# A decode attention kernel whose first key load is split into sixteen rows and the other 112

## The chip, the core and the metric

The kernel runs on one core of one Trainium2 chip. The metric is the device time of one execution in microseconds. Three runs of the kernel before took 628.09, 628.12 and 628.2 us; their median, 628.12 us, is the time before.

## The reference

The kernel computes attention of one query position over 65,536 cached keys, with 32 query heads in groups of four that share one of eight key/value heads:

```python
B, Hq, Hkv, Sq, Sk, D = 1, 32, 8, 1, 65536, 128      # all bf16
k = jnp.repeat(k, rep, axis=1)                       # rep = 4
v = jnp.repeat(v, rep, axis=1)
scores = jnp.einsum("bhqd,bhkd->bhqk", q, k) * D ** -0.5
p = _softmax(scores, axis=-1)
return jnp.einsum("bhqk,bhkd->bhqd", p, v)
```

All of K and V is read once, 134.2 MB each, and the output is 8 KB.

## The kernel before, in words

**Tiling.** One head's 65,536 keys are four units of 16,384 keys. A unit lies in SBUF as 128 partitions of T = 128 keys each, a key being 128 bf16 numbers (256 bytes), so a unit of K or of V is 4 MB, 32 KB on each partition. Two units are a pair; the sixteen pairs are the sixteen laps of every engine's loop (NP = 16). Of a pair, one partition holds 256 consecutive keys, 64 KB that are contiguous in HBM.

**What an engine does in a lap.** TensorE (PE) transposes K in blocks of eight 128x128 tiles into PSUM (`trb`, L135). VectorE (DVE) and ScalarE (ACT) copy the blocks to SBUF (`ktb`, evictions at L207 and L205). PE multiplies them with the four queries of the head (L144) into a PSUM bank of scores (`qkb`). DVE takes the maximum (L225), GpSimd (POOL) takes it over the partitions (L393), ACT makes the exponentials (L347), and PE multiplies them with V (L162) into `pvb`. The sums are rescaled from unit to unit on DVE. At the end of the last lap the last head's output is scaled, transposed and stored (L305, L191, L339, L448).

**Buffers and loads.** `kbuf` and `vbuf` hold a pair each (64 KB on each partition), `bbuf` holds the second K unit of a pair. All bulk loads are issued by SyncE (SP), in program order and through one queue: K of a pair, then V of it, lap after lap. Before it issues a K load, SP waits for `kfree`; before V, for `vfree`. In laps 1 to 13 K comes as one load of 8 MB into `kbuf`, and POOL and ACT copy its second unit into `bbuf`. In laps 0, 14 and 15 the two units are loaded apart, into `kbuf` and `bbuf`.

**The start, around the change.** In lap 0 SP issues each K unit as two pieces of 64 keys per partition (`K_PIECES = ((64, 64), (64, 64))`, L407 in `pieces`). A piece is 128 rows of 16 KB, one row on each partition, with 64 KB between the starts of two rows in HBM; it is 2 MB. Each piece has a semaphore (`kp0_0` for the first), which the load raises by 16 when it has landed. Behind the four pieces comes V of pair 0, 8 MB in one load (L437). ACT issues the load of the queries (`qsb`, 32 rows of 256 bytes, L372) on its own queue at the same time.

PE begins with 48 small matmuls on the identity (`PE_LEAD`, L184), transposes the queries when they have landed (L186), waits for the f32 identity (`t_if`), and enters its loop, where the first transposition of `kbuf` waits for `kp0_0`.

**The end.** In the last lap, K comes as two pieces for `kbuf` and one load for `bbuf`, and V as a load of 128 keys per partition and four pieces of 73, 38, 13 and 4 (L407). PE takes each piece as it lands.

## Time and profile before

| | |
|---|---|
| median of three runs | 628.12 us (628.09 to 628.2) |
| span of the profiled execution, first to last instruction | 626.9 us |
| median less that span | 1.2 us |
| PE, DVE, ACT, POOL busy | 77%, 50%, 37%, 26% of the span |
| bulk load queue (q1) busy | 99.2% of sixteen DMA engines over the span |
| HBM read | 268.44 MB, 428 GB/s over the span |

The profile gives the span of one profiled execution and no other time of it; what lies before its first and after its last instruction is seen only as the 1.2 us between the span and the median of the runs. In the rows, L numbers are lines of the kernel; a group's row has its busy time, the mean duration, and what ended the idle time ahead of it. "us to landing" of a DMA runs from its issue to the raising of its semaphore, and so includes the time that it stands in the queue behind earlier loads. In the rows of the stages, the columns after each engine's busy time are the granted clock, the DMA share and the GB/s that the DMA engines moved.

### The profile page before, as it was taken

The numbers are of one execution on the slowest core, as the hardware profiler recorded it, in microseconds if no ns is written. First come the engines' busy times: TensorE is split into PE (matmuls) and PEld (weight loads), VectorE is DVE, ScalarE is ACT, GpSimd is POOL, SyncE is SP. The second block draws the span as 40 slices with busy tenths as digits, with TensorE's granted clock in tenths as the row PEclk, the third lists the DMA queues.
The fourth block names the chain that finished last, engine by engine and source line by source line (L and its number), as shares of the span: only waits on it lengthen the run. The fifth ranks groups of instructions, "written<-read, shape, count | busy, mean of one in ns | idle before, by whom it ended". The sixth has DMA issues, their size and how long they took to land. (4 is left out here: it accounts for less than half of the span.)

```text
span 626.9 us, 27931 instructions
## 1 busy us (share of the span) xinstructions
PE 484.6 (77%) x12340; PEld 478.9 (76%) x12340; DVE 315.1 (50%) x699; ACT 228.9 (37%) x445; POOL 159.9 (26%) x124
## 2 busy tenths in 40 slices
PE   5752995959859498694976959679496894999698
PEld 5752995949859498694976959679496894999698
DVE  4620752817537174371734717356183562848274
ACT  2320532615335153341634407245062441624133
POOL 0000704307042070520605115060150702400000
PEclk9965875958769587695966959678596785969597
DMA  8999999999999999999999999999999999999997
GB/s 366 440 449 424 439 431 439 431 439 426 443 422 447 410 460 410 460 406 460 410 439 431 426 443 426 443 426 439 431 439 431 439 431 435 416 447 424 420 433 302
DMA packets 6280, 268.57 MB, mean 428 GB/s; under 512 B 896, under 2 KB 1024, under 8 KB 1152
## 3 DMA queue, kind: packets, MB, share of 16 engines
q1 hardware_dynamic: 6224, 268.45, 99.2%
q8 instruction: 6, 0.10, 0.1%
q10 hardware_dynamic: 48, 0.01, 0.0%
q14 instruction: 2, 0.02, 0.0%
HBM read 268.44 MB, written 0.01 MB: 428 GB/s over the span
## 5 line engine op out<-in xcount | busy, mean ns | idle before, releaser
L207 DVE COPY ktb<-trb 128x1024 bf16<-128x1024 bf16 x384 | 254.6, 689 | 177.5 <-PE trb L135 173.7
L205 ACT ACTIVATE ktb<-trb 128x1024 bf16<-128x1024 bf16 x128 | 131.0, 1023 | 352.7 <-PE trb L135 297.9
L135 PE MATMUL trb<-ident,kbuf 128*128 128x128 bf16 x2048 | 177.1, 245 | 104.7 <-PEq L49 104.6
L135 PEld LDWEIGHTS trb<-ident,kbuf 128*128 128x128 bf16 x2048 | 143.9, 111 | 105.6 <-issue 105.5
L213 POOL COPY bbuf<-kbuf 128x2048 bf16<-128x2048 bf16 x78 | 143.9, 1893 | 177.6 <-POOLq L49 177.6
L144 PE MATMUL qkb<-qcur,ktb 128*128 128x4 bf16 x4096 | 174.3, 165 | 11.8 <-PEq L49 10.3
L144 PEld LDWEIGHTS qkb<-qcur,ktb 128*128 128x128 bf16 x4096 | 155.2, 97 | 14.6 <-issue 14.6
L135 PE MATMUL trb<-ident,bbuf 128*128 128x128 bf16 x2048 | 157.0, 220 | 5.2 <-issue 3.9
L162 PE MATMUL pvb<-pts,vbuf 128*128 128x4 bf16 x4096 | 113.0, 166 | 15.2 <-PEq L49 11.0
L162 PEld LDWEIGHTS pvb<-pts,vbuf 128*128 128x128 bf16 x4096 | 111.1, 103 | 16.6 <-issue 15.6
L135 PEld LDWEIGHTS trb<-ident,bbuf 128*128 128x128 bf16 x2048 | 117.4, 97 | 5.5 <-issue 5.5
L393 POOL PARTITION_ALL_REDUCE cmaxa<-cmax x32 | 11.9, 370 | 254.1 <-POOLq L49 254.1
L347 ACT ACTIVATE pts<-qkb,negm 128x128 bf16<-128x128 f32 x128 | 50.9, 549 | 37.2 <-ACTq L49 37.2
L356 ACT ACTIVATE bbuf<-kbuf 128x2048 bf16<-128x2048 bf16 x26 | 49.5, 1902 | 0.0
L347 ACT ACTIVATION_READ_ACCUMULATOR pts<-qkb,negm 128x1 f32 x128 | 35.6, 278 | 0.0
L225 DVE TENSOR_REDUCE cmax<-qkb 128x4 f32<-128x512 f32 x32 | 22.0, 686 | 23.4 <-DVEq L49 23.4
L259 DVE TENSOR_TENSOR acc<-acc,pvb 128x4 f32<-128x4 f32 x16 | 2.5, 158 | 30.0 <-PE pvb L162 30.0
L257 DVE COPY acc<-pvb 128x4 f32<-128x4 f32 x8 | 1.3, 163 | 21.8 <-PE pvb L162 21.8
L395 POOL PARTITION_ALL_REDUCE la<-lp x8 | 3.4, 430 | 30.7 <-POOLq L49 30.7
L236 DVE SCALAR_TENSOR_TENSOR negm<-cmaxa,m 128x4 f32<-128x4 f32 x24 | 3.9, 163 | 11.7 <-DVEq L49 11.5
L351 ACT ACTIVATE alpha<-dm 128x4 f32<-128x4 f32 x32 | 7.1, 221 | 0.0
L250 DVE TENSOR_TENSOR acc<-acc,alpha 128x4 f32<-128x4 f32 x24 | 3.9, 164 | 6.1 <-DVEq L49 5.7
(44 smaller groups left out, 41.6 us busy)
## 6 DMA issues: line engine op xcount, KB each, us to landing
kbuf<-in_k_dram SPq DMA_DIRECT2D x4, 2048.0 KB, 16.3
bbuf<-in_k_dram SPq DMA_DIRECT2D x2, 4096.0 KB, 20.9
bbuf<-in_k_dram SPq DMA_DIRECT2D x2, 2048.0 KB, 19.9
kbuf<-in_k_dram SPq DMA_DIRECT2D x1, 4096.0 KB, 16.3
vbuf<-in_v_dram SPq DMA_DIRECT2D x1, 4096.0 KB, 21.9
vbuf<-in_v_dram SPq DMA_DIRECT2D x1, 2336.0 KB, 27.1
vbuf<-in_v_dram SPq DMA_DIRECT2D x1, 1216.0 KB, 29.6
vbuf<-in_v_dram SPq DMA_DIRECT2D x1, 416.0 KB, 30.1
```

Of the source, the lines that this page charges most:

```text
L135: ins = pe.transpose(trb[j % NTB][:, i * P:(i + 1) * P], kv[:, t, :], ident[:, :])
L144: ins = pe.matmul(qkb[n][:, t * R:(t + 1) * R], lhsT=ktb[:, off:off + P], rhs=qcur[:, :], start=True, stop=True)
L162: ins = pe.matmul(pvb[n][:, 0:R], lhsT=vv[:, t, :], rhs=pts[n][:, t * R:(t + 1) * R], start=t == 0, stop=t == T - 1)
L205: e.activation(dst, trb[j % NTB][:, :], AF.Copy).then_inc(eva, 1)
L207: e.tensor_copy(dst, trb[j % NTB][:, :]).then_inc(evd, 1)
L213: ins = op(bbuf[:, c * CB * D:(c + 1) * CB * D], kbuf[:, off:off + CB * D])
L225: e.tensor_reduce(cmax[:, :], qkb[n][:, :].rearrange("p (t g) -> p g t", g=R), AX.X, ALU.max).then_inc(cm, 1)
L236: return e.scalar_tensor_tensor(to[:, :], cmaxa[:, :], -scale, mo[:, :], ALU.mult, ALU.min)
L347: ins = e.activation(pv[:, g, :], sv[:, g, :], AF.Exp, bias=negm[:, g:g + 1], scale=scale, accum_out=rsum[:, g:g + 1])
L351: e.activation(alpha[:, :], dm[:, :], AF.Exp, scale=1.0).then_inc(sx, 1)
L356: return e.activation(o, i, AF.Copy)
L393: e.partition_all_reduce(cmaxa[:, :], cmax[:, :], P, bass.bass_isa.ReduceOp.max).then_inc(cma, 1)
```

## The change

The first piece of `kbuf` in lap 0 is issued as two loads. The first has rows (partitions) 0 to 15, 256 KB, and raises a new semaphore `kf0`; the second has rows 16 to 127, 1.75 MB, and raises `kp0_0`. Both have rows of 16 KB as before. The second piece of 64 keys is issued as before behind them. PE waits for `kf0` once, ahead of its loop, and has one identity matmul less at its start (47 for 48).

```diff
-PE_LEAD = 48
+PE_LEAD = 47
...
+FIRST = 16
...
+    kf0 = sem("kf0")
...
         pe.wait_ge(t_if, 1)
+        pe.wait_ge(kf0, 16)
         with pe.Fori(0, NP) as lap:
             pe_pair(pe, lap)
...
-                    if p == 0 or (p == NP - 1 and n == 0):
+                    if p == 0 and n == 0:
+                        w = K_PIECES[0][0] * D
+                        e.dma_start(to[0:FIRST, 0:w], s[0:FIRST, 0:w]).then_inc(kf0, 16)
+                        e.dma_start(to[FIRST:P, 0:w], s[FIRST:P, 0:w]).then_inc(kp[0][0], 16)
+                        pieces(to[:, w:W], s[:, w:W], K_PIECES[0][1:], kp[0][1:])
+                    elif p == 0 or (p == NP - 1 and n == 0):
                         pieces(to, s, K_PIECES[n], kp[n])
```

On SP's queue these are the first loads before; shapes are partitions x bf16 elements of a row:

```order
L407 DMA kbuf<-in_k_dram 128x8192 x2
L407 DMA bbuf<-in_k_dram 128x8192 x2
L437 DMA vbuf<-in_v_dram 128x32768
L418 DMA kbuf<-in_k_dram 128x32768 [waits kfree]
L437 DMA vbuf<-in_v_dram 128x32768 [waits vfree]
```

And these are the same place of SP's queue in the changed kernel:

```order
L430 DMA kbuf<-in_k_dram 16x8192
L431 DMA kbuf<-in_k_dram 112x8192
L410 DMA kbuf<-in_k_dram 128x8192
L410 DMA bbuf<-in_k_dram 128x8192 x2
L445 DMA vbuf<-in_v_dram 128x32768
L421 DMA kbuf<-in_k_dram 128x32768 [waits kfree]
```

One load of 128 rows has become one of 16 and one of 112; every load behind them stands one issue later, and nothing else on SP's queue moves.

On PE these are the first rows before, with the waits in brackets:

```order
L184 MATMUL pvb<-ident 4x4 [waits t_id]
L184 MATMUL pvb<-ident 4x4 x47
L186 MATMUL pvb<-ident,qsb 128x32 [waits q_sem]
L188 UNCONDITIONAL_BRANCH [waits t_if]
L135 MATMUL trb<-ident,kbuf 128x128 [waits kp0_0]
```

And in the changed kernel:

```order
L186 MATMUL pvb<-ident 4x4 [waits t_id]
L186 MATMUL pvb<-ident 4x4 x46
L188 MATMUL pvb<-ident,qsb 128x32 [waits q_sem]
L191 UNCONDITIONAL_BRANCH [waits kf0,t_if]
L137 MATMUL trb<-ident,kbuf 128x128 [waits kp0_0]
```

The new wait stands on the branch into the loop, directly ahead of the wait for `kp0_0` that was there before. On the other engines the order is the same.

## The prediction

> **What bounds the kernel now.** I read the page's head and its DMA rows first, to see whether any compute engine could be the limit.

> ```profile
> span 626.9 us, 27931 instructions
> ...
> PE 484.6 (77%) x12340; PEld 478.9 (76%) x12340; DVE 315.1 (50%) x699; ACT 228.9 (37%) x445; POOL 159.9 (26%) x124
> ...
> q1 hardware_dynamic: 6224, 268.45, 99.2%
> ```

> No compute engine is over 77%, and the queue of bulk loads keeps the sixteen DMA engines at 99.2% of the whole span. Next I read the stages, to see whether that holds from the first microseconds on.

> ```profile
> core 0: us, PE busy (x) PEld busy (x) DVE busy (x) ACT busy (x) POOL busy (x), PEclk, DMA share, GB/s
> ...
> 1.60:3.60 2.00, 0.34 (x14) 0.34 (x15) 1.21 (x9) 1.21 (x3) 0.00 (x0) 1.00 0.91 264
> 3.60:8.60 5.00, 1.63 (x47) 1.45 (x43) 0.59 (x4) 0.04 (x1) 0.00 (x0) 1.00 1.02 433
> ...
> 20.00:600.00 580.00, 448.18 (x11423) 443.18 (x11421) 289.62 (x631) 214.60 (x415) 157.99 (x115) 0.76 1.00 433
> ```

> From 3.6 us on the loads run at 433 GB/s, and still at 433 as a mean from 20 to 600 us, at a DMA share of 1.00. Only the first two microseconds of transfer are slower, 264 GB/s. One DMA engine therefore moves 433/16 = 27.1 GB/s, and a row of 16 KB takes it 16,384/27.1 = 0.605 us. This **row time** is the unit of what follows. A piece of 128 rows gives each engine eight of them, 4.84 us.

> Does the queue ever run empty, so that a delay at the start could be made up? The issues of the later loads answer that.

> ```profile
> vbuf<-in_v_dram SPq DMA_DIRECT2D x15, 26.8
> kbuf<-in_k_dram SPq DMA_DIRECT2D x13, 25.9
> ```

> These are loads of 8.39 MB, which need 8.39/0.433 = 19.4 us. They land 25.9 and 26.8 us after their issue (medians), so each stands some 6.5 to 7.4 us, less landing itself, behind older loads. There is no empty time into which a late start could vanish.

> Last, what the end hangs on. The chain that ended last, its first pieces and then the stretch that releases it:

> ```profile
> 620.88 2.08 PE pvb L162 x73
> 622.96 0.43 PE pvb L155 x2
> 623.39 1.59 PE pvb L162 x55
> ```
> ```profile
> 579.88 0.33 SPq L428 DMA_DIRECT2D bbuf<-in_k_dram  x1
> ```
> ```profile
> L428 SPq DMA_DIRECT2D bbuf<-in_k_dram x1: 328/328/328, 579.9 to 579.9; - x1
> ...
> DMA to landing us min/median/max: 25.1/25.1/25.1
> ```
> ```profile
> 605.28 0.61 PE L135 MATMUL trb<-ident,bbuf 128*128 128x128 bf16 x8 [1.36 <-PEq L49]
> ```

> The last K load, issued at 579.88, lands at 579.88 + 25.1 = 605.0. PE has stood idle for 1.36 us and takes up `bbuf` at 605.28; the end comes 21.6 us later, through sixteen blocks of K, the exponentials and the values.

> ```profile
> vbuf<-in_v_dram SPq DMA_DIRECT2D x1, 128.0 KB, 29.9
> ```
> ```profile
> 592.83 2.23 SPq L407 DMA_DIRECT2D vbuf<-in_v_dram  x5
> ```

> The last piece of V, issued last of the five at about 594.6, lands at about 594.6 + 29.9 = 624.5, half a microsecond before PE's last matmul ends at 623.39 + 1.59 = 624.98. Both arrivals come off the same queue. So the rule for this case is: **the time moves by as much as the slowest DMA engine falls behind or gets ahead in the first piece**, one for one.

> **The change part by part.** First the edits that I cost at nothing, with what hides them.

> ```profile
> 0.72 0.88 SPq L407 DMA_DIRECT2D kbuf<-in_k_dram  x2
> ...
> 3.26 1.34 PE L184 MATMUL pvb<-ident 128*4 128x4 bf16 x48 [3.26 <-DVE ident L325]
> ...
> 5.03 0.20 PE L186 MATMUL pvb<-ident,qsb 32*128 32x32 bf16 x1 [0.43 <-DMA qsb<-in_q_dram]
> ...
> 8.18 3.57 PE L135 MATMUL trb<-ident,kbuf 128*128 128x128 bf16 x32 [2.94 <-PEq L49]
> ```

> - *One more issue on SP.* Two issues took 0.88 us, 0.44 each. The four loads behind come 0.44 us later, and the 112 rows follow the 16 by 0.44 us. A first row takes each engine at least 0.605 us and the 112 rows another seven row times, 4.2 us, so there is always something queued: 0. Without that cover it would be 0.44.
> - *One identity matmul less.* 1.34/48 = 28 ns, ahead of a wait of 0.43 us for the queries: 0.
> - *The wait for kf0.* It stands ahead of the wait for `kp0_0`, whose 112 rows are issued later: PE is idle for 2.94 us there until 8.18 us, and only blocks of PE's loop are queued behind it. All that PE does next needs `kp0_0` too: 0. PE's own start may slip with the piece, and its idle share (23%) takes that.

> What is left is the transfer. The trace has no bulk load that covers fewer than 128 partitions, so the price of sixteen rows on sixteen neighbouring partitions must be bounded.

> - *Lower end.* If sixteen engines write sixteen neighbouring partitions as freely as 128, the 16 rows take one row time and the 112 rows seven: 0.605 + 4.235 = 4.84, as before. Loss 0. A gain could only come from the slow start: 2.0 us at 264 GB/s instead of 433 is 2.0 x (1 - 264/433) = 0.78 us lost now, and an earlier first row can win back at most that.
> - *Upper end.* The 27.1 GB/s may be the limit not of an engine but of a way into SBUF that serves eight partitions, one engine to each in a load of 128 rows. Then sixteen neighbouring rows may lie on as few as two of the sixteen ways: eight row times each, while the other ways rest. A way that rests still has its eight rows of the piece to receive, and nothing later is slack, so all the rest is lost: 8 x 0.605 = 4.84 us.
> - *Value taken.* The nearest rows lie at the ends, so I take the middle, 2.42 us, which is what four ways would cost (16/4 = 4 row times).

> [...]

> - *The 112 rows.* Seven to an engine no longer fit eight to a way, so two engines will at times write over one way, and such a row goes at half speed. From below 0, as in every 128-row load; from above, all seven rows at half speed, 7 x 0.605 = 4.2 us. I take one row time, 0.6, since the rows seen are all at full speed.
> - *The start itself.* Between 0 and -0.78; I take 0, since each engine still waits for a first row of 16 KB.

> **Sum.** 626.9 + 2.42 + 0.6 = 629.9 us of span; with the 1.2 us that lie around it, 631.1. The same 3.0 us on the median of the runs gives 628.12 + 3.02 = **631.1 us**.

> **The rivals.**

> 1. *The earlier start wins (not slower).* A load of sixteen rows is described sooner than one of 128, each engine has its first row at once, and the ways are no limit. For it: the 264 GB/s of the first two microseconds. Against it: what is slow there may be the first access itself. Price 0 to -0.78, so 627.3 to 628.1, say 627.9. It decides if the 16 rows land in less than about 3.1 us. That bound comes from this row of the loads of `kbuf` up to 12 us:

> ```profile
> DMA to landing us min/median/max: 7.3/9.5/11.7
> ```

> The first piece lands 7.3 us after its issue; less seven row times that leaves 7.3 - 4.24 = 3.1 us. With four shared ways it is 3.1 + 3 x 0.605 = 4.9 us.

> 2. *Shared, but wide.* If neighbours share eight ways, or a way is twice as fast as an engine, the loss is one row time: 628.12 + 0.6 = 628.7, up to 629.3 with a collision.

> 3. *The 112 rows are dealt out in turn.* The one load of few partitions that the trace has is that of the queries:

> ```profile
> qsb<-in_q_dram ACTq DMA_DIRECT2D x1, 8.0 KB, 4.3
> ```

> If neighbouring rows go to neighbouring engines, every round of sixteen rows lies on the same few ways: eight rounds of four row times, 19.4 us instead of 4.84, loss 14.5: 642.6. Against it, weakly: the 32 rows of the queries landed in 4.3 us, but 8 KB would not show a shared way.

> 4. *The loads are not spread as said.* If the 112 rows go to fewer engines, eight say, each has fourteen row times: 8.5 instead of 4.24, loss 4.2: 632.4.

> **How the numbers follow.** Forecast, shared ways with a loss of 1.3 to 4.9: 0.57 (629.4 to 633.0). Rival 1: 0.18. Rival 2: 0.13. Rival 3: 0.06. Rival 4: 0.06. A measurement of this kernel can tell about 0.2%, 1.26 us, from no change. Slower by more than that: forecast, rivals 3 and 4, 0.69. Within it: rival 2 and nearly all of rival 1, 0.29. Faster by more: 0.02, since 0.78 us is the most that the start holds. The range 627.6 to 633.0 takes in the forecast, rivals 2 and 4 and most of rival 1; the forecast's own is 629.4 to 633.0.

> **What would show it.** In the changed kernel the load of 256 KB should land about 4.9 us after its issue (3.1: rival 1). PE's first transposition of `kbuf`, now at 8.18, should come at about 11.2; the GB/s from 1.6 to 3.6 us should fall below 264; from 20 us on 433 must stand; and the last K load should land at about 608 instead of 605.0. I am wrong in the mechanism if the early windows are as fast as before and the end is late all the same, and wrong in size if the 16 rows land at 4.9 but the 112 take longer than eight row times behind them.

## The result, and the profile after

The changed kernel took 631.93 us (five runs, 631.6 to 632.07); the kernel before took 628.12 on the same chip (628.02 to 628.24). The ratio is 1.0059, with a 95% interval of 1.0047 to 1.0071: 3.8 us slower. The prediction was 631.1 with a range of 627.6 to 633.0.

The head of the page of the changed kernel, and its bulk queue:

```profile
span 630.6 us, 27931 instructions
...
PE 486.0 (77%) x12339; PEld 480.7 (76%) x12339; DVE 315.0 (50%) x699; ACT 228.8 (36%) x445; POOL 159.9 (25%) x124
...
q1 hardware_dynamic: 6240, 268.45, 99.2%
```

The span is 3.7 us longer, and these rows do not say where: the busy times of the compute engines differ by at most 1.8 us, and the queue is still "busy" 99.2% of sixteen engines' span. Only the page's row of GB/s in forty slices shows the place: the first slice has 269 for the 366 before. The DMA share does not show it either: in the second of the stages below it is 0.92 at little more than half the rate (243 GB/s for the 433 before). So the rate has to be read beside the share, in the stages of the changed kernel:

```profile
1.60:3.60 2.00, 0.34 (x14) 0.34 (x15) 1.21 (x9) 1.21 (x3) 0.00 (x0) 1.00 1.32 224
3.60:8.60 5.00, 1.18 (x41) 0.97 (x36) 0.59 (x4) 0.04 (x1) 0.00 (x0) 1.00 0.92 243
8.60:11.60 3.00, 0.00 (x0) 0.00 (x0) 0.00 (x0) 0.00 (x0) 0.00 (x0) 1.00 0.93 268
...
20.00:600.00 580.00, 449.56 (x11432) 444.96 (x11429) 290.25 (x632) 213.85 (x414) 157.99 (x115) 0.76 1.00 433
```

Up to 11.6 us the DMA engines move 224 to 268 GB/s at a DMA share of 0.92 or more; before, the window from 3.6 to 8.6 us had 433. From 20 us on it is 433 in both. The loads of the first piece, by their sizes, with the time from issue to landing, and PE's first transposition:

```profile
kbuf<-in_k_dram SPq DMA_DIRECT2D x1, 1792.0 KB, 10.9
kbuf<-in_k_dram SPq DMA_DIRECT2D x1, 256.0 KB, 4.7
```
```profile
12.19 2.08 PE L137 MATMUL trb<-ident,kbuf 128*128 128x128 bf16 x18 [6.34 <-PEq L50]
```

The sixteen rows land 4.7 us after their issue (the prediction had 4.9 for four shared ways, 3.1 for free ones). The 112 rows, issued at 1.2, land at 12.1, and PE starts at 12.19 instead of 8.18: 4.0 us late. What becomes of that is read at the end, from the last K load and the chain that ended last:

```profile
L436 SPq DMA_DIRECT2D bbuf<-in_k_dram x1: 328/328/328, 584.2 to 584.2; - x1
...
DMA to landing us min/median/max: 24.5/24.5/24.5
```
```profile
608.93 0.61 PE L137 MATMUL trb<-ident,bbuf 128*128 128x128 bf16 x8 [0.83 <-PEq L50]
```
```profile
624.53 2.09 PE pvb L164 x73
626.61 0.43 PE pvb L157 x2
627.04 1.57 PE pvb L164 x55
```

The last K load lands at 584.2 + 24.5 = 608.7, where it was 605.0: 3.7 us late. PE takes it up at 608.93 (605.28 before) and the chain ends as far behind. Of the 4.0 us by which PE starts late 3.7 are left at the end. The queue was never empty, as the medians of the 8 MB loads, unchanged to the tenth, show:

```profile
vbuf<-in_v_dram SPq DMA_DIRECT2D x15, 26.8
kbuf<-in_k_dram SPq DMA_DIRECT2D x13, 25.9
```

### The profile page after: what moved, and what is told of

Its sections match the earlier page's. It is cut to its first block, busy times and chain, and to the rows that moved or that the text cites. A ratio compares the mean times of both kernels' runs of the same rounds, so it can differ in the third digit from the quotient of the medians.

```text
span 630.6 us, 27931 instructions
## 1 busy us (share of the span) xinstructions
PE 486.0 (77%) x12339; PEld 480.7 (76%) x12339; DVE 315.0 (50%) x699; ACT 228.8 (36%) x445; POOL 159.9 (25%) x124
## 3 DMA queue, kind: packets, MB, share of 16 engines
q1 hardware_dynamic: 6240, 268.45, 99.2%
## 5 line engine op out<-in xcount | busy, mean ns | idle before, releaser
L137 PE MATMUL trb<-ident,kbuf 128*128 128x128 bf16 x2048 | 179.5, 247 | 107.3 <-PEq L50 107.3
L137 PEld LDWEIGHTS trb<-ident,kbuf 128*128 128x128 bf16 x2048 | 145.5, 112 | 108.3 <-issue 108.1
L146 PEld LDWEIGHTS qkb<-qcur,ktb 128*128 128x128 bf16 x4096 | 156.3, 97 | 14.5 <-issue 14.5
L164 PE MATMUL pvb<-pts,vbuf 128*128 128x4 bf16 x4096 | 112.7, 166 | 15.3 <-PEq L50 11.2
L239 DVE SCALAR_TENSOR_TENSOR negm<-cmaxa,m 128x4 f32<-128x4 f32 x24 | 3.9, 163 | 11.7 <-DVEq L50 11.5
## 6 DMA issues: line engine op xcount, KB each, us to landing
vbuf<-in_v_dram SPq DMA_DIRECT2D x1, 2336.0 KB, 27.1
kbuf<-in_k_dram SPq DMA_DIRECT2D x1, 1792.0 KB, 10.9
```

The costliest lines, as they stand in the source:

```text
L137: ins = pe.transpose(trb[j % NTB][:, i * P:(i + 1) * P], kv[:, t, :], ident[:, :])
L146: ins = pe.matmul(qkb[n][:, t * R:(t + 1) * R], lhsT=ktb[:, off:off + P], rhs=qcur[:, :], start=True, stop=True)
L164: ins = pe.matmul(pvb[n][:, 0:R], lhsT=vv[:, t, :], rhs=pts[n][:, t * R:(t + 1) * R], start=t == 0, stop=t == T - 1)
L239: return e.scalar_tensor_tensor(to[:, :], cmaxa[:, :], -scale, mo[:, :], ALU.mult, ALU.min)
```

## The experiments

Every edit below is in SP's code for the first piece of `kbuf` in lap 0, against the changed kernel, unless said otherwise. Each ran beside the kernel before.

### The same two sizes, cut by columns

```diff
-e.dma_start(to[0:FIRST, 0:w], s[0:FIRST, 0:w]).then_inc(kf0, 16)
-e.dma_start(to[FIRST:P, 0:w], s[FIRST:P, 0:w]).then_inc(kp[0][0], 16)
+c = FIRST // 2 * D
+e.dma_start(to[:, 0:c], s[:, 0:c]).then_inc(kf0, 16)
+e.dma_start(to[:, c:w], s[:, c:w]).then_inc(kp[0][0], 16)
```

> The first piece of 2 MB is again issued as two loads, of 256 KB and 1.75 MB, but cut by columns: 128 rows of 2 KB, then 128 rows of 14 KB. Theory (shared ways: the loss comes from loads that cover few or unevenly many partitions): both loads cover all 128 partitions, so no loss: 628.1 us, within 0.5, at most 0.78 earlier. Rival A (what costs is the extra load itself: its issue, its descriptors, its completion): as the changed kernel, about 631.9. Rival B (HBM reads: what costs is which rows of HBM are read together): the rows read together are those of the kernel before, so 628.1 as well; this run does not tell B from the theory.

Measured: 628.33 us beside 628.2, ratio 1.0 (0.9991 to 1.0009). A second load of 256 KB ahead of the rest costs nothing when it covers all partitions; the extra issue and the wait for `kf0` are in this run as well. Nor does it gain anything. Its early stages:

```profile
1.60:3.60 2.00, 0.34 (x14) 0.34 (x15) 1.20 (x9) 1.21 (x3) 0.00 (x0) 1.00 0.95 307
3.60:8.60 5.00, 1.38 (x44) 1.27 (x40) 0.59 (x4) 0.04 (x1) 0.00 (x0) 1.00 1.01 423
```

The first window is faster than before (307 GB/s for 264), the next one slower (423 for 433), and PE starts at 8.33 instead of 8.18.

### Eight loads of sixteen neighbours, and eight of sixteen spread partitions

```diff
+for i in range(8):
+    r = slice(i * FIRST, (i + 1) * FIRST)
+    e.dma_start(to[r, 0:w], s[r, 0:w]).then_inc(kf0 if i < 7 else kp[0][0], 16)
```

> The first piece is issued as eight loads of sixteen neighbouring rows. Theory: each load lies on four of sixteen ways, so it takes four row times of 0.605 us; eight of them 19.4 us instead of 4.84: 628.1 + 14.5 = 642.6 us. Rival A (each extra load costs 3.8 us, as the one extra load of the changed kernel): 628.1 + 7 x 3.8 = 654.7. If rows of few partitions were free and only the 112 rows cost: 628.1 to 629.

```diff
-    e.dma_start(to[r, 0:w], s[r, 0:w]).then_inc(kf0 if i < 7 else kp[0][0], 16)
+    e.dma_start(to[i:P:8, 0:w], s[r, 0:w]).then_inc(kf0 if i < 7 else kp[0][0], 16)
```

> As the eight loads of sixteen rows, with the same rows read from HBM in the same order, but written to partitions i, i+8, i+16 and so on. The keys then lie on other partitions than their values, so the output is another one; the bytes moved are the same. Theory: sixteen partitions at a step of eight reach eight ways, two rows each, so a load takes two row times, eight loads 9.7 us instead of 4.84: 628.1 + 4.8 = 633.0 us. Rival B (HBM reads): the reads are those of the run beside it, so the same time as that one. Rival A: 654.7, as that one.

Measured: 639.94 us for the neighbours (ratio 1.0192, 1.0176 to 1.0207), 633.16 for the spread ones (1.0079, 1.0064 to 1.0094), beside 628.2. So +11.7 and +5.0. The two differ in nothing but the partitions that they write; the same rows are read from HBM in the same order. That is against rival B, and against rival A too, which had 654.7 for both. The spread loads came out as the theory had it (4.8). The neighbours lost less than the 14.5 that it gave. One stage from the middle of those loads:

```profile
6.00:16.00 10.00, 0.15 (x1) 0.04 (x1) 0.59 (x4) 0.00 (x0) 0.00 (x0) 1.00 0.98 120
```

Sixteen rows are 262 KB, at 120 GB/s 2.18 us, where four row times are 2.42. The kind of cost is right and its size is 10% too high for these loads, of which each lies on other partitions than the one before it.

### The time of a load by its shape

```diff
+for c in cols:                      # the kernel before, ahead of its first load; c: a quarter of vbuf
+    e.dma_start(vbuf[0:P, c], vq[0:P, c]).then_inc(probe, 16)
+e.wait_ge(probe, 64)
+for c in cols:
+    e.dma_start(vbuf[16:P, c], vq[16:P, c]).then_inc(probe, 16)
+e.wait_ge(probe, 128)
...
```

> Ahead of the kernel before, SP issues nine groups of four loads of 16 KB rows into quarters of vbuf (all overwritten later) and waits for each group; the time of one load of a group is (landing of the fourth less landing of the first) / 3. Theory, row time 0.605 us: 128 rows 4.84 us; 112 rows (partitions 16 to 127) about 6.8, as the changed kernel's trace shows; the same 112 partitions from contiguous HBM rows 6.8 too; 112 rows on partitions 0 to 111 also over 4.9; 64 rows on partitions 0 to 63 4.84 (eight ways); 32 rows on 0 to 31 2.42 (eight ways); 16 rows on 0 to 15 2.42 (four ways); 16 rows at a step of eight 1.21; 64 rows at a step of two between 2.42 and 4.84. Without shared ways: 128 rows 4.84, 112 4.24, 64 2.42, 32 1.21, 16 0.605, whatever the step. Rival B (HBM reads): the 112 rows from contiguous HBM take another time than the 112 rows 64 KB apart, and 16 rows take the same at both steps.

> Again groups of four loads of 16 KB rows ahead of the kernel before; the time of one load is (landing of the fourth less landing of the first) / 3. The question is why 112 rows take 6.7 us where the fullest way has only eight rows to take, 4.84. Theory C: the rows are dealt to the engines in runs of neighbours, so that engines meet on a way while other ways rest. Worked through by hand for such runs with ways shared evenly: 112 rows about 6.4 (6.7 was measured), 96 rows on partitions 0 to 95 6.4, 96 on 32 to 127 7.3, 48 on 0 to 47 4.6 to 4.84. Theory D: only the fullest way counts, and 112 has a cost of its own: 96 rows 4.84 both times, 48 rows 4.84. No shared ways: 3.63, 3.63, 1.8. Controls by the ways alone: 32 rows at a step of four on all partitions 1.21 to 2.42; 64 rows on 64 to 127 4.84 to 5.0, as on 0 to 63; 64 odd rows 2.42, as the even ones; 16 rows at a step of four on partitions 0 to 63 1.21 (eight ways).

The rows of three of the groups in the first of these runs (128 rows, 112 rows, 16 rows on partitions 0 to 15) give the first and last issue of the four, then the shortest and the longest time to landing:

```profile
L419 SPq DMA_DIRECT2D vbuf<-in_v_dram x4: 412/416/694, 0.7 to 2.1; - x4
...
DMA to landing us min/median/max: 7.3/13.9/20.5
```
```profile
L422 SPq DMA_DIRECT2D vbuf<-in_v_dram x4: 342/428/483, 22.7 to 24.0; - x4
...
DMA to landing us min/median/max: 8.9/18.8/27.7
```
```profile
L437 SPq DMA_DIRECT2D vbuf<-in_v_dram x4: 311/420/421, 148.6 to 149.9; - x4
...
DMA to landing us min/median/max: 4.7/7.7/10.0
```

These two runs (one execution each) took 807.14 and 762.36 us in all, as the groups stand ahead of everything else. For 112 rows the first lands at 22.7 + 8.9 = 31.6 and the fourth at 24.0 + 27.7 = 51.7, so one takes 20.1/3 = 6.7 us. All groups, worked out in the same way, in us for one load:

| rows of 16 KB on partitions | free rows would take | measured |
|---|---|---|
| 128: all | 4.84 | 4.87 |
| 64: 0 to 63; 64 to 127 | 2.42 | 5.03; 5.03 |
| 64: even; odd | 2.42 | 2.43; 2.43 |
| 32: 0 to 31 | 1.21 | 2.43 |
| 32: every fourth of 128 | 1.21 | 1.40 |
| 16: 0 to 15 | 0.605 | 2.20 |
| 16: every eighth of 128; every fourth of 0 to 63 | 0.605 | 1.23; 1.20 |
| 112: 16 to 127; 0 to 111 | 4.24 | 6.70; 6.73 |
| 112: 16 to 127, rows contiguous in HBM | 4.24 | 6.97 |
| 96: 0 to 95; 32 to 127 | 3.63 | 6.73; 6.80 |
| 48: 0 to 47 | 1.82 | 5.33 |

The fourth load of a group, with none of its group behind it, lands sooner than the others in some groups, so some of these means are low: the landings of the sixteen rows on 0 to 15 are 2.41, 2.41 and 1.78 us apart, those of the 112 rows on 16 to 127 are 7.01, 7.03 and 6.08. In the changed kernel itself the 112 rows land at 1.2 + 10.9 = 12.1 and the sixteen at 0.7 + 4.7 = 5.4, 6.7 apart.

The last three columns of stages in the middle of five of the groups (128; 112; 64 on partitions 0 to 63; 32 on 0 to 31; 64 even) say the same as rates:

```profile
6.00:18.00 12.00, 0.00 (x0) 0.00 (x0) 0.09 (x1) 0.00 (x0) 0.00 (x0) 1.00 1.02 436
30.00:46.00 16.00, 0.00 (x0) 0.00 (x0) 0.00 (x0) 0.00 (x0) 0.00 (x0) 1.00 1.01 278
...
116.00:132.00 16.00, 0.00 (x0) 0.00 (x0) 0.00 (x0) 0.00 (x0) 0.00 (x0) 1.00 1.01 207
138.00:146.00 8.00, 0.00 (x0) 0.00 (x0) 0.00 (x0) 0.00 (x0) 0.00 (x0) 1.00 1.04 215
...
170.00:177.00 7.00, 0.00 (x0) 0.00 (x0) 0.00 (x0) 0.00 (x0) 0.00 (x0) 1.00 1.01 433
```

Partitions 0 to 63 take rows at 207 GB/s and 0 to 31 at 215, half the rate of all 128, while 64 even partitions take them at 433, with the same rows of HBM read as for 0 to 63. It is not how many partitions a load has but which. In row times of 0.605 us, sixteen neighbours (0 to 15) take four where the four loads stand in the queue together (2.41 us from landing to landing), 32 (0 to 31) take no more (2.43), 64 (0 to 63) about eight (5.03), and all 128 no more than those 64 (4.87). The controls go the same way: 0 to 63 at the rate of 0 to 31, the even partitions at the full rate, sixteen at a step of eight nearly twice as fast as sixteen neighbours (1.23 for 2.20). All of these but the even partitions, for which it gave a range, are within 10% of what the theory had by its counts of ways; that rows meet on ways is inferred from these times.

The 112 rows take 6.7 us from HBM rows 64 KB apart and 6.97 from contiguous ones, so the reads do not make them slow. And they take more than the fullest way needs by the theory (eight rows, 4.84). The 96 rows do so too, twice: that is nearer to theory C of the second run (6.4 and 7.3 expected, 6.73 and 6.80 measured) than to D (4.84 both times), but the 0.9 us by which the two were to differ is not there. The 48 rows took 5.33, above what either gave.

The packets kept in the trace, one to a row of 16 KB, go against C as well. In the middle of the group of 128 rows each takes 0.61 us, and in that of 0 to 63 between 1.25 and 1.29, near the two row times (1.21) of the theory. Of the 271 that start in the stage of the 112 rows (30 to 46 us) none is under 0.70 or over 1.40, and half are under 0.93; in the middle of the groups of 96 rows none is under 0.95, and in that of 48 rows each takes 1.78 to 1.92. If engines met on some ways while the others ran free, with each way shared evenly, over half of the rows in a load of 112 or 96 would meet nobody and take about 0.6: that is an estimate, worked out from the row time and runs of neighbours. So all engines are slowed about alike, and C has a sum that is nearly right without the picture behind it.

### The sixteen rows alone

```diff
+spare = sb("spare", [P, 64 * D], DT.bfloat16)
...
-e.dma_start(to[0:FIRST, 0:w], s[0:FIRST, 0:w]).then_inc(kf0, 16)
-e.dma_start(to[FIRST:P, 0:w], s[FIRST:P, 0:w]).then_inc(kp[0][0], 16)
+e.dma_start(spare[0:FIRST, 0:w], s[0:FIRST, 0:w]).then_inc(kf0, 16)
+e.dma_start(to[:, 0:w], s[:, 0:w]).then_inc(kp[0][0], 16)
```

> The load of sixteen rows stays ahead, but into a spare buffer that nothing reads, and the piece itself comes as one load of 128 rows: the sixteen rows are moved twice, and no load has 112 rows. Theory: the sixteen rows cost 2.1 to 2.4 us on their four ways (2.12 was one row's time in the run of eight such loads), and the 128 rows nothing more: 628.2 + 2.1 to 2.4 = 630.3 to 630.6 us. Without shared ways the extra row of each engine costs 0.6: 628.8. If the sixteen rows were the whole loss of the changed kernel, 628.2 + 3.8 + 0.6 = 632.6.

Measured: 630.2 us beside 628.24, ratio 1.0036 (1.0022 to 1.005), +1.96, just under what the theory had. One row more for each engine is 0.605 by the row time, so the sharing of ways by the sixteen rows is put at 1.96 - 0.605 = 1.36 us, an estimate. It is only a part of the 3.8.

### Halves, and even and odd partitions

```diff
+e.dma_start(to[0:64, 0:w], s[0:64, 0:w]).then_inc(kf0, 16)
+e.dma_start(to[64:P, 0:w], s[64:P, 0:w]).then_inc(kp[0][0], 16)
```

> The first piece as two loads of 64 rows, partitions 0 to 63 and 64 to 127. Theory: each half lies on eight of the sixteen ways, eight rows to a way, 4.84 us each (5.0 in the run of shapes): 628.2 + 4.5 to 5.0 = 632.7 to 633.2 us. Rival A (a load that covers fewer than 128 partitions costs something of its own, whichever they are): the same time as the run with even and odd partitions.

```diff
+e.dma_start(to[0:P:2, 0:w], s[0:P:2, 0:w]).then_inc(kf0, 16)
+e.dma_start(to[1:P:2, 0:w], s[1:P:2, 0:w]).then_inc(kp[0][0], 16)
```

> The first piece as two loads of 64 rows, even partitions and odd partitions: the same two loads, rows and bytes as the halves, but each load reaches all sixteen ways with four rows each. Theory: 2 x 2.42 = 4.84, no loss: 628.2 us within 0.4. Rival A: as the halves, 633.

Measured: 633.4 us for the halves (ratio 1.0084, 1.0067 to 1.01), 628.5 for even and odd (1.0004, 0.9995 to 1.0013), beside 628.24. Two loads of 64 rows each, the same bytes, issues and waits: +5.2 and +0.3. Rival A is out. The 5.2 is what the table gives, 2 x 5.03 - 4.87 = 5.19.

### The 112 rows as seven loads at a step of seven

```diff
-e.dma_start(to[FIRST:P, 0:w], s[FIRST:P, 0:w]).then_inc(kp[0][0], 16)
+for i in range(7):
+    r = slice(FIRST + i, P, 7)
+    e.dma_start(to[r, 0:w], s[r, 0:w]).then_inc(kf0 if i < 6 else kp[0][0], 16)
```

> The sixteen rows stay ahead as in the changed kernel; the other 112 rows come as seven loads of sixteen rows at a step of seven, partitions 16, 23, ..., 121, then 17, 24, ..., 122, and so on. A load of sixteen rows gives one row to each engine, so each engine gets a run of seven neighbouring partitions, one after the other. Theory C (the load of 112 rows is dealt to the engines in such runs, and its loss is engines meeting on a way): each engine then has the same rows in the same order as in the changed kernel, so the same time, 631.9 us within 0.5, though there are seven loads instead of one. If 112 rows had a cost of their own, these seven loads would not have it: a load reaches ten or more ways with at most two rows on one, so with engines free to run ahead between 4.84 and 8.5 us for the seven, and nothing that ties it to 6.7. If the 112 rows were dealt in turn, this order would be far better than theirs, which their 6.7 us already speaks against. Rival A (each extra load costs): 628.2 + 7 x 3.8 = 654.8.

Measured: 632.04 us beside 628.21, ratio 1.0058 (1.0045 to 1.0072); the changed kernel's was 1.0059. The stages from 3.6 to 11.6 us are those of the changed kernel (243 and 268 GB/s there):

```profile
3.60:8.60 5.00, 1.19 (x41) 0.98 (x37) 0.60 (x4) 0.05 (x1) 0.00 (x0) 1.00 0.93 243
8.60:11.60 3.00, 0.00 (x0) 0.00 (x0) 0.00 (x0) 0.00 (x0) 0.00 (x0) 1.00 0.97 262
```

Here the deal is made in the program: if the sixteen rows of each load go to the sixteen engines in order, which no view shows, an engine gets seven neighbouring partitions one after the other. That it costs the same as the one load of 112 rows, to 0.1 us, speaks against a cost of 112 rows in one load and for one part of theory C, that the load is dealt in runs of seven neighbours, though the 4.84 to 8.5 us expected without that hold 6.7 as well. It does not show how the loss comes about: the rows are slowed alike here too (none under 0.72 us from 4 to 11 us).

## Why the prediction was right, and what it mis-sized

- **What bounds it**: right, and "one for one" nearly so. Of the 4.0 us by which the first piece came late 3.7 were left at the last K load and in the span.
- **The edits at nothing**: right. The run cut by columns has the additional issue, the wait and the 47 matmuls, and costs nothing that can be measured.
- **Shared ways**: right in kind. Loads that differ only in the partitions that they write go from +5.0 to +11.7 us; even and odd partitions against halves, which also group the reads in another way, from +0.3 to +5.2. Of the signs that were named, the sixteen rows landed at 4.7 us (4.9 forecast), the first window fell to 224 GB/s, PE's first transposition came at 12.19 us (about 11.2 forecast), 433 stood from 20 us on, and the last K load landed at 608.7 (about 608 forecast).
- **The sum** is where the size was off, by 0.8 us: +3.0 forecast, +3.8 measured. The time of the first piece was forecast as four row times for the sixteen rows (2.42) and, for the 112, eight for the fullest way and one for collisions (5.44): 7.86 us. Measured are 1.96 for the sixteen rows and 6.70 for the 112, together 8.66. Less 4.84 this is 3.82, and the kernel lost 3.81. So the step that was mis-sized is the last one, "I take one row time, 0.6, since the rows seen are all at full speed": what the prediction put down to collisions cost 6.70 - 4.84 = 1.86, three row times. The prediction's own sign for this came true: the 112 rows took longer than eight row times (4.84) behind the sixteen, 6.7 us. The 0.46 by which the sixteen rows were dearer on paper hid a part of it, and that was luck. That the 2.42 is near was luck in part too: it was taken as the middle of two bounds. Four row times is what the sixteen rows need when load after load lies on the same sixteen partitions (2.41 from landing to landing).
- **Rival 1, the earlier start**: nothing of the 0.78 us came. Cut by columns or in even and odd rows, a smaller first load gained no time (628.33 and 628.5). In the run cut by columns the load of 256 KB landed 2.9 us after its issue, inside the 3.1 of this rival, and still nothing was gained. So a smaller first load does not cure what is slow in the first two microseconds; what it is was not tried.
- **Rival 2**, shared but wide, had at most +1.2 us. The kernel lost 3.8, and sixteen neighbours, which this rival would have at two row times (1.21), took 2.20 in the table.
- **Rivals 3 and 4**: the 112 rows do not go in turn. Dealt so, their rounds would be the neighbours of the eight loads at +11.7. Nor do they go to eight engines: the group of 112 rows moved 278 GB/s, and eight engines at 27.1 would move 217.

What stays open is how the 1.86 us of the 112 rows come about. No view names the engine of a row, so the runs of neighbours are inferred, and why all engines are slowed alike was not tried. And the runs do not hold for all loads: runs of eight among 128 rows, or of four among the 64 even ones, would by the theory meet on the ways too, and these run at 436 and 433 GB/s. How those are dealt was not tried.

## What to carry to other kernels

Where one queue of loads sets the time and never runs empty, a slow load at the start is paid almost in full at the end (3.7 of 4.0 us here), and a DMA share near 1 does not show it (0.92 at 243 GB/s here): read the GB/s beside it. Which partitions a load writes decided its rate here: 436 GB/s for all 128 and 433 for every second one, 207 for 0 to 63 and 278 for 16 to 127. If a piece must come in two loads, cut it by columns, or into even and odd partitions, which cost 0.1 to 0.3 us here, within the noise; cut into neighbouring partitions it cost 3.8 (16 and 112) and 5.2 (64 and 64).

## What had not been expected

The eight loads of sixteen neighbours moved 120 GB/s, which would be 30 for each of the theory's four ways, more than the 27.1 of one engine (433/16). But each of those loads lies on other partitions than the one before it. Where four loads in a row lay on the same sixteen partitions, the rows on 0 to 15 took 2.41 us a load, by that count 4 x 16,384 bytes in 2.41 us or 27.2 GB/s a way, as much as one engine moves where all 128 partitions are written. That engines which are ahead were already on the partitions of the next load, and so moved the 120, would fit but was not tried. The 64 rows on 0 to 63, by the theory two engines on each of eight ways, moved 207, 25.9 a way, a little less, and why was not settled. And 48 rows on neighbouring partitions take 5.33 us, longer than 64 rows (5.03).
